# A spectral mixer and token MLP on one core: first transform copied out of PSUM two tiles at a time, in a hand-written order, with fixed PSUM banks and smaller units in the middle

## Chip, cores, metric

The kernel runs on one core of a Trainium2 chip. The metric is the device time of one execution in microseconds (us), median of several runs; lower is better. The profile's span is some 1.5 to 1.8 us shorter than the device time and starts with the first instruction. PSUM is the memory, in eight banks, into which PE writes its results. Engines: PE multiplies matrices, DVE (VectorE), ACT (ScalarE) and POOL (GpSimd) work elementwise, SP issues most loads.

## The reference

```python
x = A_x                                           # [1, 2048, 512], bf16
h = x + A(layernorm(x), w_r, w_i)                 # A: rfft2 over (2048, 512), times W = w_r + i w_i, irfft2
h2 = h + B(layernorm(h), w1, b1, w2, b2)          # B: gelu(h^T w1 + b1) w2 + b2 over the 2048 tokens, F = 1376
```

## The kernel before

The Fourier transforms are products with constant matrices. The stages that matter here, with the program's names:

- **Front.** Sixteen tiles X (128 x 512) are loaded. The mean goes away by itself in the transform; the norm factor rs is made per tile (DVE or ACT), and the constant FP is scaled by it into FS (POOL, ACT or DVE). f1 = four matmuls per tile into PSUM (ps); Y = copy of ps to SBUF.
- **Middle**, eight units of four groups: f2 (matmuls on Y, result copied to CS), x (matmuls on CS), V = ps times W (DVE, reading PSUM), g1 (matmuls on V, result copied to PQ by ACT).
- **Residual stage**, sixteen tiles: g2, EO copy, g3, then on DVE two residual adds (TT), H, and HH = normalised H; ACT makes squares (JK) and the factor r.
- **Two large products** on PE with GELU between (w1, w2), until the end.

A small list scheduler in the kernel orders all instructions: it takes, again and again, the operation that can start first by its estimates of durations, and picks a PSUM bank for it. Only this order is compiled; each engine works off its own list strictly in that order. Besides the real matmuls, PE's list of the front holds 32 on a tile of zeros, called fillers or zero matmuls here: they keep PE busy so that its granted clock stays full (what happens without them is seen in e3 below).

```python
N_WARM = 20                                         # matmuls on a tile of zeros before the first real one
WARM_AFTER = (4, 3, 2, 1, 1, 0, 1, 0, ...)          # and behind tile 0, 1, 2 ... of the first transform
...
for q in range(8):                                  # front: per pair of tiles and half b, one copy of 512
    for b in range(2):
        unit = PsumUnit("f1", 1)
        for n in range(2):
            mm(f"f1_{n2}_{b}a", ...); mm(f"f1_{n2}_{b}b", ...)
        if (q, b) in Y_DVE: dve(f"y_{q}_{b}", ... tensor_copy ..., 512, prio=28)
        else:               act(f"y_{q}_{b}", dst, src, ACT.Copy, 512, prio=28)
        ... warm(f"warmf{q}{n}{w_}", wu, 13, after=[lastmm[n]])
...
def stage_x(u):                                     # middle: eight matmuls, then V in one or two operations
    unit = PsumUnit("x", 2)
    grp = [cs_ops[2 * u + 1]]
    ...
    nh = 2 if u in V_SPLIT else 1                   # V_SPLIT = (0, 7)
...
def act(...):
    return K.op(name, "act", emit, ..., occ=lat - 90.0, lat=lat + 50.0, ...)   # the scheduler's estimate for ACT
```

Of the kernel before, what the change touches and what calls it, by code (L numbers as in the profile page):

```python
# [6 lines left out]
ACT = mybir.ActivationFunctionType  # L7
ALU = mybir.AluOpType
LN_EPS = 1e-5
NP = 128  # L10
S_LEN = 2048
D_LEN = 512
# [24 lines left out]
def _row(sign, comp, k2, s):  # L37
    return 4 * (k2 * 2 + s) + 2 * sign + comp
# [52 lines left out]
def build_consts():  # L91
# [22 lines left out]
    fp = fp.reshape(NP, NS2, NP)  # L114
    fp = np.stack([-fp, fp], axis=2)
# [26 lines left out]
    c["E"] = e.reshape(NP, 1024)  # L142
    c["MR"] = np.concatenate([m.reshape(NP, 512), r.reshape(NP, 512)], axis=1)
# [5 lines left out]
PSUM_BANKS = 8  # L149
CELL = 4  # L150
# [28 lines left out]
class Builder:  # L179
    def __init__(self, nc, limits):  # L180
        self.nc = nc
        self.ops = []
        self.writer = {}
        self.readers = {}
        self.tensors = {}
        self.limits = limits
        self.cell_cache = {}

# [37 lines left out]
    def op(self, name, engine, emit, ins=(), outs=(), occ=100.0, lat=None, unit=None, pr=False, pw=False,  # L226
           first=False, last=False, prio=0, nbytes=0, is_dma=False, not_before=0.0, after=(), group=None, rate=DMA_RATE):
# [13 lines left out]
        o.rate = rate  # L241
        deps = {id(d): d for d in after}
# [38 lines left out]
    def schedule(self):  # L281
# [13 lines left out]
        order = []  # L295
        while len(order) < len(ops):
            best = None
            for o in ready:
                bank, avail = None, 0.0
                u = o.unit  # L300
                if u is not None and not u.claimed:
# [5 lines left out]
                    for b in range(PSUM_BANKS - u.nbanks + 1):  # L307
                        if all(bank_unit[i] is None for i in range(b, b + u.nbanks)):
                            t = max(bank_free[b:b + u.nbanks])
                            if cand is None or t < cand[0]:  # L310
                                cand = (t, b)
# [10 lines left out]
            ready.remove(o)  # L322
            o.sched, o.start = True, st
# [11 lines left out]
            if o.is_dma:  # L335
                x0 = max(st + (3200.0 if st < 4000.0 else 1700.0), dma_free)
                dma_free = x0 + o.bytes / o.rate
                o.finish = dma_free + 200.0
            else:
                o.finish = st + o.lat  # L340
# [86 lines left out]
def memory_layout():  # L427
# [26 lines left out]
    add("W", [NP, NG, 2, LW], bf, rw)  # L454
    add("HH", [NP, NS2, D_LEN], bf, rw)
# [29 lines left out]
RS_GROUPS = ((0,), (2,), (4,), (5,), (6, 7), (8, 9), (10, 11), (12,), (13,), (14,), (15,))  # L485
FS_ENG = {4: "act", 7: "act", 9: "dve", 11: "dve", 13: "dve", 14: "act", 15: "dve"}
Y_DVE = ((5, 1), (6, 1), (7, 1))
N_WARM = 20
WARM_AFTER = (4, 3, 2, 1, 1, 0, 1, 0, 0, 0, 0, 0, 0, 0, 0, 0)
V_SPLIT = (0, 7)  # L490
# [4 lines left out]
def build_kernel(nc, A_x, A_w_r, A_w_i, B_w1, B_b1, B_w2, B_b2, out):  # L495
# [5 lines left out]
    K = Builder(nc, {"f1": 6, "f2": 2, "x": 2, "g1": 2, "g2": 2, "g3": 2, "mm1": 5, "mm1b": 6, "mm2": 8})  # L501
# [3 lines left out]
    X, FS, Y, CS, V, PQ, EO, H, HH, GT, OUT, W = (T[n] for n in ("X", "FS", "Y", "CS", "V", "PQ", "EO", "H", "HH", "GT", "OUT", "W"))  # L505
# [9 lines left out]
    def dma(name, dst, src, nbytes, stream="sp", outs=(), ins=(), prio=0, strided=False, after=(), group=None, rate=DMA_RATE,  # L515
            not_before=0.0):
        def emit(eng, bank):
            if strided:
                with nc.allow_non_contiguous_dma(reason="small bias gather"):
# [3 lines left out]
                    rate=rate, occ=1000.0 if stream == "pool" else 640.0 if rate < DMA_RATE else 460.0, not_before=not_before)  # L523
# [10 lines left out]
    def act(name, dst, src, func, n, ins=(), outs=None, unit=None, prio=0, last=True, psum=True, bias=None, scale=None, accum=None):  # L534
# [15 lines left out]
        return K.op(name, "act", emit, ins=ii, outs=oo, occ=lat - 90.0, lat=lat + 50.0, unit=unit, pr=unit is not None,  # L550
# [13 lines left out]
    def ldf(q, pr_, stream="sp", nb=0.0):  # L564
        sl = slice(4 * q, 4 * q + 4)
        dma(f"ld_FP{q}", FP[:, sl, :, :], cin[f"FP{q}"][:, :, :, :], 1 << 18, outs=[FP[:, sl, :, :]], prio=pr_, stream=stream, not_before=nb)

    for q, (a, b) in enumerate(((0, 2), (2, 4), (4, 6), (6, 8), (8, 12))):
        ldx(a, b, 90 - q)
    ldf(2, 84)  # L570
    ldx(12, 16, 83)
    ldf(3, 82)
    ldf(0, 90, "act")
    act("table", T["tb"][:, 0:1], EPS[:, 0:1], ACT.Abs_reciprocal_sqrt, 1, ins=[EPS[:, 0:1]], prio=88)
    ldf(1, 87, "act", 1800.0)
    dma("ld_E", EM[:, 0:1024], cin["E"][:, :], 1 << 18, outs=[EM[:, 0:1024]], prio=44)
    dma("ld_MR", EM[:, 1024:2048], cin["MR"][:, :], 1 << 18, outs=[EM[:, 1024:2048]], prio=43)
    wload = {}
    for ch, (u0, u1) in enumerate(((0, 1), (1, 4), (4, 8))):
        g0, ng = 4 * u0, 4 * (u1 - u0)  # L580
        lst = []
        for w, dram in ((0, A_w_r), (1, A_w_i)):
            for comp in range(2):
                d = W[comp::4, g0:g0 + ng, w, :]
                lst.append(dma(f"ld_wp{ch}_{w}{comp}", d, bass.AP(dram.tensor, g0 * LW, [[64 * LW, 32], [LW, ng], [1, LW]]),
                               32 * ng * 514, prio=42 - ch, group=f"w{ch}", rate=300.0))
                h0, nh = (g0, ng) if g0 else (1, ng - 1)
                d = W[2 + comp::4, h0:h0 + nh, w, :]
                lst.append(dma(f"ld_wm{ch}_{w}{comp}", d, bass.AP(dram.tensor, (64 - h0) * LW, [[64 * LW, 32], [-LW, nh], [1, LW]]),
                               32 * nh * 514, prio=42 - ch, group=f"w{ch}", rate=300.0))  # L590
                if g0 == 0:
                    d = W[2 + comp::4, 0, w, :]
                    lst.append(dma(f"ld_wz{ch}_{w}{comp}", d, bass.AP(dram.tensor, 32 * LW, [[64 * LW, 32], [1, LW]]),
                                   32 * 514, prio=42 - ch, group=f"w{ch}", rate=300.0))
        for u in range(u0, u1):
            wload[u] = lst
    dma("ld_D2", EM[:, 2048:3072], cin["D2"][:, :], 1 << 18, outs=[EM[:, 2048:3072]], prio=30)
    dma("ld_IF", IF[:], cin["IF"][:, :, :], 1 << 19, outs=[IF[:]], prio=29)
    w1src = B_w1.rearrange("(p s2) f -> p s2 f", s2=NS2)
    for q in range(4):  # L600
        sl = slice(4 * q, 4 * q + 4)
        dma(f"ld_w1_{q}", W1[:, sl, :], w1src[:, sl, :], 4 * F_LEN * 2 * NP, outs=[W1[:, sl, :]], prio=28 - q, after=wload[7][-1:])
# [13 lines left out]
    ZT, BV = T["ZT"], T["bv"]  # L616
    K.op("zt", "dve", lambda eng, bank: eng.memset(ZT[:, :], 0.0), outs=[ZT[:, :]], occ=200.0, prio=60)  # L617
# [9 lines left out]
    def fs_op(i):  # L627
        e = FS_ENG.get(i, "pool")
        rs = RS[:, i:i + 1]
        if e == "act":  # L630
            act(f"fs{i}", FS[:, i, :, :], FP[:, i, :, :], ACT.Copy, 256, ins=[FP[:, i, :, :]], scale=rs, prio=30)
        else:
            dve(f"fs{i}", lambda eng, bank: eng.tensor_scalar(FS[:, i, :, :], FP[:, i, :, :], rs, None, op0=ALU.mult),  # L633
                [FP[:, i, :, :], rs], [FS[:, i, :, :]], 120, prio=30, engine=e, lat=920.0 if e == "pool" else None)

    def stat_act(i):
# [3 lines left out]
        nm = NM[:, i:i + 1]  # L640
        dve(f"nm_{i}", lambda eng, bank: eng.tensor_scalar(nm, SM[:, i:i + 1], -1.0 / D_LEN, None, op0=ALU.mult), [SM[:, i:i + 1]], [nm], 1, prio=33, engine="pool", lat=210.0)
        dve(f"bv_{i}", lambda eng, bank: eng.tensor_scalar(BV[:, i:i + 1], nm, nm, LN_EPS, op0=ALU.mult, op1=ALU.subtract), [nm], [BV[:, i:i + 1]], 1, prio=33, engine="pool", lat=210.0)
        act(f"rs_{i}", RS[:, i:i + 1], V1[:, i:i + 1], ACT.Abs_reciprocal_sqrt, 1, ins=[V1[:, i:i + 1]], bias=BV[:, i:i + 1],
            scale=-1.0 / D_LEN, prio=32)
        fs_op(i)

    def stat_dve(grp):
        a, b = grp[0], grp[-1] + 1
        for i in grp:
# [3 lines left out]
            dve(f"st_{i}", lambda eng, bank, i=i, x=x: eng.bn_stats(ST[:, i, 0:6], x), [x], [ST[:, i, 0:6]], 512, prio=25)  # L653
# [15 lines left out]
    Yv = Y[:].rearrange("p b y g (n k) -> p b (y g) n k", k=4)  # L669
    for q in range(8):  # L670
        for b in range(2):
            unit = PsumUnit("f1", 1)
            lastmm = {}
            for n in range(2):
                n2 = 2 * q + n
                lo = X[:, n2, b * NP:b * NP + NP]
                hi = X[:, n2, 256 + b * NP:256 + b * NP + NP]
                f = FS[:, n2, 1, :]
                f2 = bass.AP(f.tensor, f.offset, [list(f.ap[0]), [0, 2], [1, NP]])
                fm = FS[:, n2, :, :]  # L680

                def o(bank, n=n):
                    return ps[:, bank, n * 256:n * 256 + 256]
                mm(f"f1_{n2}_{b}a", o, lo, f2, unit, True, False, n == 0, 14, 256, ins=[lo, f])
                lastmm[n] = mm(f"f1_{n2}_{b}b", o, hi, fm, unit, False, True, False, 14, 256)

            def src(bank):
                v = ps[:, bank, :].rearrange("p (n g k) -> p n g k", n=2, k=4)
                return v.rearrange("p n g k -> p g n k")
            dst = Yv[:, b, :, 2 * q:2 * q + 2, :]  # L690
            if (q, b) in Y_DVE:
                dve(f"y_{q}_{b}", lambda eng, bank, dst=dst, src=src: eng.tensor_copy(dst, src(bank)), [], [dst], 512, unit=unit, prio=28)
            else:
                act(f"y_{q}_{b}", dst, src, ACT.Copy, 512, unit=unit, prio=28)
            for n in range(2):
                for w_ in range(WARM_AFTER[2 * q + n] if b == 1 else 0):
                    warm(f"warmf{q}{n}{w_}", wu, 13, after=[lastmm[n]], last=2 * q + n == LAST_WARM)
# [3 lines left out]
    def stage_f2(u):  # L701
        for i in range(2):
            G = 2 * u + i
            unit = PsumUnit("f2", 1)
            for par in range(2):
                for b in range(2):
                    mm(f"f2_{G}_{par}{b}", lambda bank, par=par: ps[:, bank, par * 256:par * 256 + 256],
                       Y[:, b, par, 2 * G:2 * G + 2, :].rearrange("p g k -> p (g k)"), E[:, b, par, :],
                       unit, b == 0, b == 1, par == 0 and b == 0, 10, 256)
            dst = CS[:, G, :, :, :].rearrange("p y c j -> p (y c j)")  # L710
            if G == 1:
                cs_ops[G] = dve(f"cs_{G}", lambda eng, bank, dst=dst: eng.tensor_copy(dst, ps[:, bank, :]), [], [dst], 512, unit=unit, prio=14)
            else:
# [167 lines left out]
```

## Time and profile before

| | us |
|---|---|
| device time, median (lowest to highest) of the 4 runs beside the changed kernel | 134.07 (133.96 to 134.32) |
| traced span | 132.36 |
| first V starts | 21.49 |
| V stage (first V to end of last V) | 17.88 |
| from there to the first residual add | 3.27 |
| first residual add to last HH (its start) | 26.25 |
| last HH to the end | 63.47 |

The five rows below the span add up to it; they come from the list of single instructions. (The table in the prediction was cut where the chain changes engine, so its last two stretches differ from these.) The chain of waits and the table by stretch stand in the prediction. The granted clock is 1.00 in all stretches of the prediction's table.

### The profile page before, as it was taken

How to read it: one execution, taken by the hardware profiler on the slowest of the kernel's cores; microseconds unless marked ns; L12 is line 12 of the kernel's file. 1: busy time of each engine (PE TensorE's matmuls, PEld its weight loads, DVE VectorE, ACT ScalarE, POOL GpSimd, SP SyncE). 2: the span in 40 equal slices, each digit the busy share in tenths (PEclk: the TensorE clock that was granted, in tenths of full speed). 3: DMA queues.
4: the chain of work that ended last, by engine and by line, in shares of the span. 5: the costliest groups of instructions: out<-in, count | busy, mean ns of one | idle time of the engine just before them, and what ended most of it. 6: DMA issues, size and time to landing. Idle time of an engine off the chain costs nothing.

```text
span 132.4 us, 2013 instructions
## 1 busy us (share of the span) xinstructions
PE 123.7 (93%) x776; PEld 74.5 (56%) x786; DVE 69.3 (52%) x127; ACT 63.3 (48%) x146; POOL 12.4 (9%) x33
## 2 busy tenths in 40 slices
PE   6989989999977979999999999999999999999990
PEld 2436656788666736544434444456666666666660
DVE  0499867999981999999960000000242332423322
ACT  4579976978966999986689322222000000000000
POOL 0199920000300000000000000000000000000000
PEclk9999999999999999999999999999999999999999
DMA  2999699999999999992000000000111112111121
GB/s 80 375 396 364 153 244 273 286 322 283 419 426 417 410 408 411 417 295 74 0 0 0 0 0 0 5 0 0 40 40 70 49 40 82 42 57 62 40 79 40
DMA packets 16648, 22.16 MB, mean 167 GB/s; under 512 B 2720, under 2 KB 12960, under 8 KB 16128
## 3 DMA queue, kind: packets, MB, share of 16 engines
q1 hardware_dynamic: 16352, 21.52, 47.5%
q10 hardware_dynamic: 288, 0.52, 1.1%
q8 instruction: 6, 0.10, 0.3%
q14 instruction: 2, 0.02, 0.0%
HBM read 19.95 MB, written 2.10 MB: 167 GB/s over the span
## 4 chain that ended last, share of the span: by engine, by line
PE 51%; DVE 32%; ACT 9%; DMA 3%; POOL 2%; issue 1%; DVEq 0%; ACTq 0%
PE ps L531 50%; DVE V L739 13%; DVE H L799 7%; ACT Y L549 5%; DVE TT L790 4%; DVE TT L792 4%; DVE HH L804 4%; DMA X<-in_A_x_dram 3%; POOL FS L633 1%; ACT rs L549 1%; ACT FS L549 1%; ACT JK L549 1%; DVE OUT L829 1%; ACT PQ L549 0%; PE ps L621 0%
## 5 line engine op out<-in xcount | busy, mean ns | idle before, releaser
L531 PE MATMUL ps<-HH,W 128*128 128x512 bf16 (+1 forms) x173 | 40.3, 379 | 1.3 <-DVE HH L804 0.9
L531 PE MATMUL ps<-GT,W 128*128 128x512 bf16 (+1 forms) x172 | 37.9, 379 | 0.2
L829 DVE SCALAR_TENSOR_TENSOR OUT<-ps,B2f,H 128x512 bf16<-128x512 f32 x16 | 12.0, 750 | 48.7 <-PE ps L531 48.7
L531 PEld LDWEIGHTS ps<-GT,W 128*128 128x128 bf16 (+1 forms) x176 | 25.3, 144 | 12.8
L531 PEld LDWEIGHTS ps<-HH,W 128*128 128x128 bf16 (+1 forms) x176 | 17.2, 100 | 21.2 <-DVE HH L804 1.9
L739 DVE TENSOR_TENSOR V<-ps,W 128x2048 bf16<-128x2048 f32 (+1 forms) x10 | 17.9, 1856 | 0.9 <-PE ps L531 0.9
L549 ACT ACTIVATE GT<-ps,B1f 128x512 bf16<-128x512 f32 (+1 forms) x11 | 7.1, 689 | 14.6 <-PE ps L531 14.6
L549 ACT ACTIVATE JK<-H,nm 128x512 bf16<-128x512 bf16 x16 | 11.6, 722 | 3.0 <-DVE H L799 2.9
L653 DVE BATCH_NORM_STATS2 st<-X 128x6 f32<-128x512 bf16 x14 | 9.2, 669 | 4.1 <-DMA X<-in_A_x_dram 4.1
L621 PE MATMUL ps<-ZT 128*128 128x512 bf16 x32 | 9.6, 434 | 1.6 <-DVE ZT L617 1.2
L799 DVE TENSOR_TENSOR H<-ps,TT 128x512 bf16<-128x512 f32 x16 | 10.9, 682 | 0.0
L549 ACT ACTIVATE PQ<-ps 128x512 bf16<-128x512 f32 x16 | 8.9, 602 | 3.5 <-PE ps L531 3.3
L531 PE MATMUL ps<-EM,PQ 128*128 128x256 bf16 x64 | 9.0, 273 | 0.8 <-ACT PQ L549 0.7
L531 PE MATMUL ps<-EM,V 128*128 128x128 bf16 x128 | 9.2, 219 | 0.5 <-DVE V L739 0.5
L549 ACT ACTIVATE EO<-ps 128x512 bf16<-128x512 f32 x16 | 9.2, 596 | 0.9 <-PE ps L531 0.9
L549 ACT ACTIVATE CS<-ps 128x512 bf16<-128x512 f32 x15 | 8.3, 607 | 2.1 <-PE ps L531 2.1
L531 PE MATMUL ps<-EM,Y 128*128 128x256 bf16 x64 | 8.7, 273 | 0.4 <-ACT Y L549 0.4
L531 PE MATMUL ps<-FS,X 128*128 128x256 bf16 x64 | 8.4, 274 | 0.5 <-POOL FS L633 0.4
L531 PEld LDWEIGHTS ps<-EM,V 128*128 128x128 bf16 x128 | 7.5, 98 | 2.3 <-issue 1.4
L633 POOL TENSOR_SCALAR FS<-FP,rs 128x256 bf16<-128x256 bf16 x9 | 8.6, 965 | 0.6 <-ACT rs L549 0.5
L790 DVE TENSOR_TENSOR TT<-ps,X 128x256 f32<-128x256 f32 x16 | 6.7, 417 | 3.3 <-PE ps L531 3.3
L531 PEld LDWEIGHTS ps<-EM,PQ 128*128 128x128 bf16 x64 | 6.2, 98 | 2.9 <-ACT PQ L549 0.9
(36 smaller groups left out, 79.1 us busy)
## 6 DMA issues: line engine op xcount, KB each, us to landing
W<-in_B_w_dram SPq DMA_DIRECT2D x4, 1376.0 KB, 11.7
W<-in_B_w_dram SPq DMA_DIRECT2D x10, 512.0 KB, 18.3
out_dram<-OUT SPq DMA_DIRECT2D x16, 128.0 KB, 1.7
W<-in_A_w_r_dram SPq DMA_DIRECT2D x4, 257.0 KB, 4.5
W<-in_A_w_i_dram SPq DMA_DIRECT2D x4, 257.0 KB, 5.0
X<-in_A_x_dram SPq DMA_DIRECT2D x4, 256.0 KB, 5.0
X<-in_A_x_dram SPq DMA_DIRECT2D x2, 512.0 KB, 6.6
W<-in_A_w_r_dram SPq DMA_DIRECT2D x4, 192.8 KB, 3.3
```

What stands on the lines that cost most here:

```text
L531: return K.op(name, "pe", lambda eng, bank: eng.matmul(outf(bank), lhsT, rhs, start=start, stop=stop), ins=ins or [lhsT, rhs], occ=occ, la ...
L549: return eng.activation(dst, s, func, **kw)
L621: return K.op(name, "pe", lambda eng, bank: eng.matmul(ps[:, bank, :], ZT[:, 0:NP], ZT[:, :], start=True, stop=True), ins=[ZT[:, :]], occ= ...
L633: dve(f"fs{i}", lambda eng, bank: eng.tensor_scalar(FS[:, i, :, :], FP[:, i, :, :], rs, None, op0=ALU.mult), [FP[:, i, :, :], rs], [FS[:, ...
L653: dve(f"st_{i}", lambda eng, bank, i=i, x=x: eng.bn_stats(ST[:, i, 0:6], x), [x], [ST[:, i, 0:6]], 512, prio=25)
L739: return eng.tensor_tensor(vout, s, win, ALU.mult)
L790: dve(f"tl_{s2}", lambda eng, bank, tt=tt, xl=xl: eng.tensor_tensor(tt[:, 0, :], ps[:, bank, 256:512], xl, ALU.add), [xl], [tt[:, 0, :]], ...
L792: dve(f"th_{s2}", lambda eng, bank, tt=tt, xh=xh: eng.tensor_tensor(tt[:, 1, :], xh, ps[:, bank, 256:512], ALU.subtract), [xh], [tt[:, 1, ...
L799: return eng.tensor_tensor(hs.rearrange("p (h d) -> p h d", h=2), e, tt[:, :, :], ALU.add)
L804: dve(f"hh_{s2}", lambda eng, bank, s2=s2, hs=hs: eng.tensor_scalar(HH[:, s2, :], hs, NM[:, s2:s2 + 1], R2[:, s2:s2 + 1], op0=ALU.add, op1 ...
L829: dve(f"fin{s2}", lambda eng, bank, dst=dst, bia=bia, hs=hs: eng.scalar_tensor_tensor(dst, ps[:, bank, :], bia, hs, op0=ALU.add, op1=ALU.add),
```

## The change

The intent: copies out of PSUM of two tiles at once (fewer, larger ACT operations), an order of the front written by hand, a shorter way from the last Y copy to the first V (half copies, four x matmuls, V of 512), half copies for the last unit, fewer load issues, and PSUM banks fixed by class so that stages don't block each other. The cut below leaves out that the scheduler's estimates of loads changed as well, and that the norm of the two tiles done on ACT needs one POOL step less.

```diff
+CLASS_BANKS = {"x": (4, 6), "f2": (0, 1, 2, 3), "g1": (0, 1, 2, 3)}
...
-RS_GROUPS = (..., (6, 7), (8, 9), (10, 11), (12,), (13,), (14,), (15,))
-FS_ENG = {4: "act", 7: "act", 9: "dve", 11: "dve", 13: "dve", 14: "act", 15: "dve"}
-Y_DVE = ((5, 1), (6, 1), (7, 1))
+RS_GROUPS = (..., (6, 7), (8,), (9, 10), (11, 12), (13,), (14, 15))
+FS_ENG = {3: "act", 4: "act", 9: "dve", 11: "dve", 13: "dve", 14: "dve", 15: "dve"}
+Y_EVAC = (("pair", "act"), ("pair", "act"), ("pair", "act"), _AA, ("pair", "act"), ("single", ("act",), ("dve",)), _AA, ("single", ("act",), ("dve", "act")))
+FRONT = {"dve": "bn_0 ag_0 bn_2 ...", "act": "s1_1 s2_1 rs_0 ... yp_0 rs_6 yp_1 rs_8 yp_2 ...", "pool": "...",
+         "pe": "f1_0 f1_1 f1_3 f1_4 f1_2 f1_5 ..."}
 N_WARM = 20
 WARM_AFTER = (4, 3, 2, 1, 1, 0, 1, 0, 0, 0, 0, 0, 0, 0, 0, 0)
-V_SPLIT = (0, 7)
+V_SPLIT = (7,)
...
+    K.forced = {e: FRONT[e].split() for e in ("dve", "act", "pool")}      # the scheduler must keep this order
+    K.forced["pe"] = [f"{n}_{b}{h}" for n in FRONT["pe"].split() for b in range(2) for h in "ab"]
...
-        return K.op(name, "act", emit, ..., occ=lat - 90.0, ...)
+        return K.op(name, "act", emit, ..., occ=lat - 120.0, ...)
...
+    dma("ld_EMR", ...)                              # one load instead of two
+    # first W chunk: own tile W0, 8 issues instead of 12; w1 in eight parts, D2 and IF in two
...
+            split = u == 0                          # stage_f2: CS of unit 0 in halves, ACT and DVE
+            if i == 0 or u == 0:                    # stage_x: unit 0 in two groups of four x matmuls,
+                    K.op(f"v_0_{i}{w}", "dve", ...) #          V of unit 0 from W0 in four operations of 512
+            split = (u, h) == (7, 1)                # stage_g1: last PQ copy in halves, DVE and ACT
...
+    for j, n2 in enumerate(f1_order):
+        for w_ in range(WARM_AFTER[j]):
+            warm(f"warmf{j}{w_}", wu, 13, after=[lastmm[n2]])
```

## The prediction

> **What bounds the kernel now.** I read the chain that ended last first, then the table of busy time by stretch, cut where the chain changes engine, and then the groups with shapes kept apart. The chain, in order of time (start us, us, what):
>
> ```profile
> 8.76 0.31 POOL bv L642
> ...
> 17.10 1.47 ACT Y L549 x3
> 18.57 0.05 issue
> 18.62 2.77 PE ps L531 x25
> ...
> 21.48 1.04 DVE V L739
> ...
> 22.62 15.62 DVE V L739 x8
> ...
> 40.13 0.61 ACT PQ L549
> 40.74 0.05 issue
> 40.78 1.82 PE ps L531 x14
> ```
>
> From 9.15 us on ACT holds the chain until its last Y copy at 18.57; then PE (with a CS copy inside) until 21.48; then the ten V multiplies on DVE. The table by stretch (us, then each engine's busy us):
>
> ```profile
> 9.35:18.62 9.27, 8.70 (x65) 5.61 (x65) 8.28 (x26) 9.18 (x25) 7.67 (x14) 1.00 0.90 271
> 18.62:21.48 2.86, 2.86 (x27) 2.00 (x28) 1.00 (x2) 1.69 (x3) 0.00 (x0) 1.00 0.92 241
> 21.48:39.37 17.89, 16.92 (x224) 13.01 (x223) 17.88 (x10) 14.04 (x27) 1.22 (x7) 1.00 1.08 339
> 39.37:42.63 3.26, 2.57 (x25) 2.05 (x25) 0.00 (x0) 2.04 (x5) 0.00 (x0) 1.00 1.02 427
> 42.63:68.05 25.42, 24.10 (x133) 12.73 (x134) 25.33 (x63) 22.01 (x60) 0.00 (x0) 1.00 0.71 267
> 68.05:132.40 64.35, 60.87 (x277) 35.90 (x282) 12.42 (x17) 9.17 (x15) 0.00 (x0) 1.00 0.10 33
> ```
>
> So the bound moves: ACT (9.18 of 9.27), a hand-over of 2.86, DVE (17.88 of 17.89), a hand-over of 3.26, DVE (25.33 of 25.42), PE. The change touches the first four stretches, 39.4 us. The other 90 us (residual adds and norm on DVE, the two large products on PE) keep instructions and sizes; they can only start earlier. The forms that matter:
>
> ```profile
> L739 DVE TENSOR_TENSOR V<-ps,W 128x2048 bf16<-128x2048 f32 x6 | 13.3, 2281 | 0.0
> L549 ACT ACTIVATE Y<-ps 128x512 bf16<-128x512 f32 x13 | 7.0, 607 | 0.0
> L739 DVE TENSOR_TENSOR V<-ps,W 128x1024 bf16<-128x1024 f32 x4 | 4.7, 1218 | 0.9 <-PE ps L531 0.9
> L692 DVE CAST Y<-ps 128x512 bf16<-128x512 f32 x3 | 2.1, 692 | 0.7 <-PE ps L531 0.6
> ```
>
> These durations overlap their neighbours. What counts in a full queue is the step from start to start in the list of single instructions: Y on ACT 0.478 us, V of 2048 elements 2.197, V of 1024 1.13, a one-column ACT op 0.185, FS on ACT 0.40, FS on POOL 0.925 (1.0 beside a DVE FS).
>
> **What the Trainium skill says.** (1) "Perfetto Trace Analysis", Optimizing Scalar/DVE Operations, gives an access overhead per instruction of about 51 ns for Scalar and 125 ns for DVE on PSUM, and says that larger operations help a saturated engine. ACT agrees: 0.478 - 512/1.2 GHz (0.427) = 0.051. DVE shows half: 2.197 - 2048/0.96 GHz (2.133) = 0.064; I use 0.064. (2) The same section says that where Scalar or Vector is not saturated but makes bubbles on others, smaller instructions let work finish sooner. The stretches 18.62 to 21.48 and 39.37 to 42.63 are that case: ACT is busy 1.69 of 2.86 and 2.04 of 3.26 us. (3) "VectorE: DVE Perf Modes", Why PSUM operands drop a tier, holds fp32 PSUM inputs to one element per cycle; the 2.197 us agree, so a new layout of V cannot make a V op faster per element. (4) "TensorE: Matmul & The Clock Gate", Why this matters for your kernels, warns of PE gaps over about 3 us; the granted clock is 1.00 in every stretch here.
>
> **The change, part by part.**
>
> *Y copies.* Before: 13 on ACT and 3 on DVE of 512. After, from the order of instructions: on ACT four of 1024, six of 512 and one of 256; on DVE one of 512 and one of 256. ACT gets 4x1024 + 6x512 + 256 = 7424 elements instead of 6656: 768 x 0.833 ns = 0.64 us more, less two fixed parts (0.10). One FS leaves ACT (-0.40) and one small rs op too (-0.19). Net about zero. So pairing in itself does not shorten ACT's queue; what could is ACT starting on Y earlier.
>
> It does start earlier. POOL's bv now follows directly on sm, so one POOL step is gone, and the second norm of the ACT pair finishes at about 8.24 us instead of 9.45. Walking the new order with the steps above (semaphores at what the trace shows: 0.034 us ACT to DVE, 0.09 ACT to POOL, 0.055 to PE, 0.04 from PE): FS 3 and 4 on ACT at 8.27 and 8.98, pairs at 9.57, 10.66 and 11.75, singles of tiles 6 and 7 at 12.84 and 13.31. Then ACT waits. POOL's FS of tile 8 ends at 13.4 (POOL runs without a gap from 7.8), its matmuls at 14.35, and the pair of tiles 8 and 9 starts at 14.39 instead of 13.98. Single 10 at 15.54; 12, after POOL's FS at 15.33, at 16.03; the joined rs of 14 and 15 at 16.51. FS 14 and 15 on DVE at 16.85 and 17.05, their matmuls until 17.8 and 18.2, single 14 at 17.83, and the two halves of tile 15 end at 18.47 (DVE) and 18.70 (ACT). Before, the last two copies ended at 18.57 and 18.94 (DVE). **The front ends only about 0.24 us earlier**: the early start is spent on waits, and fewer, larger pieces make each wait longer.
>
> *First middle unit.* Before: last Y copy 18.94, V at 21.485: 2.55 us, for 15 matmuls, a 512 DVE copy and eight x matmuls. After: the first half-group's matmuls end 0.33 and 0.44 us after the last copy; a 256 copy on DVE lasts 0.69 - 256/0.96 GHz = 0.42; PE reaches the first four x matmuls at +1.0 (eight f2 at 0.109, then the 0.2 us that the trace shows between f2 and x), and V comes 0.53 later (0.75 for eight x before, less two steps of 0.11). Sum 1.58, **a gain of 0.96**. First V at 18.70 + 1.58 = 20.28.
>
> *V stage.* Four V of 512 (0.597 each) replace two of 1024 (1.13): +0.13. V of unit 1 needs 13 more f2 and eight x after the second small unit; on PE's order it is ready at about 22.85, and DVE is free at 22.67: +0.2. Then six steps and two halves as before. The last V ends at about 38.5 (before 39.365): **0.2 to 0.4 lost** of the gain.
>
> *Last unit.* The last g1 result is evacuated in halves on DVE and ACT: the half on ACT takes 0.597 - 256/1.2 GHz = 0.38 instead of 0.60: **-0.21**.
>
> *Loads.* The first W chunk goes out in 8 issues of about 0.64 us instead of 12, and E, M and R as one: SP is about 3 us earlier with what follows. No V waits for W now, and W1 is needed no earlier than its gain. Off the path.
>
> Sum: -0.24 - 0.96 + 0.13 + 0.2 - 0.21 = -1.08; with some 0.1 for PE waits in the V stage, -1.0 us. The 90 us after it move as a block: **134.13 - 1.0 = 133.1 us**.
>
> **The rivals.** *PE becomes the bound of the middle.* At the first V, PE has done 12 of 64 f2 and 4 of 64 x; before it was 21 and 8. So 9 x 0.109 + 0.25 = 1.2 us of PE work moves into a stretch that DVE filled by itself. Up to its last x, PE has 64 f2 (7.0), 8 x groups (0.55 each, 4.4) and 96 g1 (0.056 each, 5.4): 16.8 us from f2's start, against about 18.4 us from there to the last unit's V. It fits, but x of unit 5 comes close: I count 12.0 us of PE work ahead of it, and it is wanted at about 12.3. Waits of 0.2 to 0.6 could add up: 133.3 to 133.7. For it speaks that V of unit 6 already waited for x (step 2.262, not 2.197); against it, that f2's order was chosen anew for this.
>
> *The front goes better or worse than my walk.* Runs of four bf16 elements in the single copies are new, and so are the strides across banks in the pairs. If ACT or DVE slowed for that by a fifth, six singles cost 0.6 us: 133.7. If the waits at tiles 8 and 14 close up, the front gains another 0.6: 132.5. POOL, the slowest per tile, makes that unlikely, since tile 12 still needs its ninth FS.
>
> *The gain is hidden.* If a W chunk or W1 were late, the earlier start would meet a DMA wait: 134. The waits show no DMA ahead of V or of the large product, and the loads go out earlier as well.
>
> **Range and chances.** Front +-0.3, hand-over +-0.2, V stage +0.5 or -0.2, and the three runs before spread by 0.36: 132.3 to 133.9 holds it 8 times in 10. Faster by over 2% means below 131.4, which needs 1.7 us more than any part offers: 0.05. Slower by 2% (136.8) needs a stage that breaks, such as a clock drop: 0.02.
>
> **What would show it.** Right: last Y copy at 18.5 to 18.9 with ACT waiting for PE before the pair of tiles 8 and 9; a first V of 512 elements near 20.3; DVE without gaps over 0.3 us until 38.5; first residual add near 41.6; stretches after it as long as before. Wrong: Y steps over 0.5 per 512 elements, an x or g1 wait of DVE in mid-stage adding to more than 0.6, a V that waits for W0, a granted clock below 1, or a DVE stage after 41.6 unlike 25.4 us.

## The result, and the profile after

The changed kernel is correct. Four runs of it took 135.34 to 136.35 us, median 136.11; the four runs of the kernel before on the same chip 133.96 to 134.32, median 134.07. The ratio is 1.014, 95% interval 1.0095 to 1.0184. A ratio here is the mean time of one kernel's fast runs over that of the other's fast runs of the same rounds, so it is not quite the ratio of the medians. The kernel is slower, and 136.11 lies outside my range of 132.3 to 133.9.

| us | before | after | difference | predicted |
|---|---|---|---|---|
| end of last Y copy | 18.94 | 20.21 | +1.27 | -0.24 |
| from there to first V | 2.55 | 1.74 | -0.81 | -0.96 |
| V stage | 17.88 | 18.60 | +0.72 | +0.43 |
| to the first residual add | 3.27 | 3.13 | -0.14 | -0.21 |
| first residual add to last HH | 26.25 | 26.89 | +0.64 | 0 |
| last HH to the end | 63.47 | 63.61 | +0.14 | 0 |
| traced span | 132.36 | 134.18 | +1.82 | -1.0 |

The same cuts in the table of busy time by stretch of the changed kernel (us; then each engine's busy us with the number of instructions for PE, PE's weight loads, DVE, ACT, POOL; then granted clock, DMA share, GB/s):

```profile
9.93:20.21 10.28, 8.99 (x66) 5.89 (x66) 7.21 (x24) 8.46 (x17) 6.87 (x14) 1.00 1.15 325
20.21:21.95 1.74, 1.74 (x16) 0.92 (x15) 0.86 (x3) 0.71 (x2) 0.00 (x0) 1.00 1.21 291
21.95:40.54 18.59, 18.06 (x236) 14.08 (x234) 18.21 (x12) 14.97 (x29) 1.28 (x7) 1.00 1.05 346
40.54:43.67 3.13, 2.65 (x26) 2.07 (x25) 0.43 (x2) 1.84 (x5) 0.00 (x0) 1.00 1.02 418
43.67:70.56 26.89, 25.58 (x140) 12.79 (x139) 25.68 (x63) 22.99 (x63) 0.00 (x0) 1.00 0.58 207
70.56:134.18 63.62, 60.30 (x279) 35.58 (x277) 12.44 (x17) 8.39 (x12) 0.00 (x0) 1.00 0.10 33
```

ACT, which filled the front before (9.18 of 9.27), now is busy 8.46 of 10.28: it waits. In the V stage PE is as full (18.06 of 18.59) as DVE. The residual stage has the same instructions and 0.64 us more.

One caution on the first row. The first zero matmuls take 0.427 us each, and from some moment on 0.216; call this the full clock. It came at 4.13 us in the trace before and at 6.25 in the one after. In a1 below, which has the same front as the changed kernel, it came at 3.99, and the last Y copy ended at 19.73 instead of 20.21: so some 0.5 us hangs on that moment. Two later runs with the old front and the new loads ended it at 18.62 (d1, full clock at 4.09) and 19.02 (e1, 6.24). At like clocks the new front is thus 1.1 to 1.2 us later than the old one, so the 1.27 isn't luck.

The chain of waits of the changed kernel, in order of time (start us, us, what), tells what ACT waits for. Line 648 is the helper of the zero matmuls, line 553 that of all real ones:

```profile
1.17 6.97 PE ps L648 x20
8.14 0.45 PE ps L553 x4
8.63 0.82 PE ps L648 x3
9.45 0.44 PE ps L553 x4
9.89 0.88 PE ps L648 x4
10.77 1.32 PE ps L553 x12
12.12 1.02 ACT Y L571
...
20.12 13.51 PE ps L553 x163
33.66 4.50 DVE V L824 x2
```

The chain begins with PE, not with ACT: 20 zero matmuls, 4 real ones, 3 zero, 4 real, 4 zero, 12 real, and only then ACT's second pair copy at 12.12. My walk had that copy at 10.66. From 20.12 to 33.66 the chain stays on PE, where the kernel before had DVE's V. The kernel before has fillers between the first tiles too (PE's list, line 621 the zero ones):

```profile
7.52 0.61 PE L531 MATMUL ps<-FS,X 128*128 128x256 bf16 x4 [0.42 <-POOL FS L633]
8.19 0.82 PE L621 MATMUL ps<-ZT 128*128 128x512 bf16 x3
8.85 0.60 PE L531 MATMUL ps<-FS,X 128*128 128x256 bf16 x4
9.28 0.83 PE L621 MATMUL ps<-ZT 128*128 128x512 bf16 x3
10.03 0.61 PE L531 MATMUL ps<-FS,X 128*128 128x256 bf16 x4
```

There they cost little: leaving them out brought the first V only 0.3 us forward (b3 and d3 below).

### The profile page after: what moved, and what is told of

Same layout as the page of the kernel before. It is cut to its first block, busy times and chain, and to the rows that moved or that the text cites. A ratio compares the mean times of both kernels' runs of the same rounds, so it can differ in the third digit from the quotient of the medians.

```text
span 134.2 us, 2029 instructions
## 1 busy us (share of the span) xinstructions
PE 126.0 (94%) x786; PEld 74.9 (56%) x786; DVE 69.8 (52%) x131; ACT 63.6 (47%) x143; POOL 12.1 (9%) x32
## 4 chain that ended last, share of the span: by engine, by line
PE 69%; DVE 14%; ACT 12%; issue 3%
PE ps L553 62%; PE ps L648 7%; ACT JK L571 4%; DVE H L899 4%; DVE V L824 3%; ACT Y L571 3%; ACT EO L571 3%; DVE HH L904 2%; DVE TT L890 2%; DVE TT L892 2%; ACT r L571 1%; ACT PQ L571 1%; DVE OUT L929 1%; ACT rs L571 1%; DVE FS L660 0%
## 5 line engine op out<-in xcount | busy, mean ns | idle before, releaser
L553 PE MATMUL ps<-HH,W 128*128 128x512 bf16 (+1 forms) x176 | 41.0, 379 | 1.3 <-DVE HH L904 1.1
L824 DVE TENSOR_TENSOR V<-ps,W 128x2048 bf16<-128x2048 f32 (+1 forms) x8 | 15.7, 2019 | 0.4 <-PE ps L553 0.2
L648 PE MATMUL ps<-ZT 128*128 128x512 bf16 x34 | 11.0, 467 | 1.4 <-DVE ZT L591 1.2
L571 ACT ACTIVATE PQ<-ps 128x512 bf16<-128x512 f32 (+1 forms) x16 | 9.1, 590 | 3.7 <-PE ps L553 3.6
L571 ACT ACTIVATE CS<-ps 128x512 bf16<-128x512 f32 (+1 forms) x16 | 8.4, 575 | 1.5 <-PE ps L553 1.5
L571 ACT ACTIVATE Y<-ps 128x512 bf16<-128x512 f32 (+2 forms) x11 | 7.7, 731 | 2.2 <-PE ps L553 2.2
L553 PEld LDWEIGHTS ps<-FS,X 128*128 128x128 bf16 x64 | 5.9, 98 | 3.7 <-DVE FS L660 2.0
```

What stands on the lines that cost most here:

```text
L553: return K.op(name, "pe", lambda eng, bank: eng.matmul(outf(bank), lhsT, rhs, start=start, stop=stop), ins=ins or [lhsT, rhs], occ=occ, la ...
L571: return eng.activation(dst, s, func, **kw)
L648: return K.op(name, "pe", lambda eng, bank: eng.matmul(ps[:, bank, :], ZT[:, 0:NP], ZT[:, :], start=True, stop=True), ins=[ZT[:, :]], occ= ...
L824: return eng.tensor_tensor(vout, s, win, ALU.mult)
```

## The experiments

My theory after the two traces had three parts. (1) The zero matmuls stand in PE's list ahead of real ones, so the hand-written order of the front comes late. (2) The small first unit moves PE work behind the first V and makes DVE wait in the V stage. (3) The scheduler, with another estimate for ACT, wrote another order in the residual stage. The rivals: the new copies are slower (excluded at once by the trace: the pair of 1024 takes 1.02 us, and pairs follow each other after 1.09 as in my walk; the singles step by 0.478 as before), the fixed banks cause the waits, or the loads do. All times are medians, with the lowest and highest run in brackets; the ratio is to the kernel before in the same rounds. Except for c2, which is wrong, every kernel was correct.

| run | time | ratio [95%] |
|---|---|---|
| changed kernel | 136.11 (135.34 to 136.35) | 1.0140 [1.0095, 1.0184] |
| a1_stage_order | 135.44 (134.53 to 135.65) | 1.0100 [1.0063, 1.0137] |
| a2_warm14 | 135.27 (135.17 to 135.30) | 1.0095 [1.0069, 1.0122] |
| a3_nowarm | 134.44 (134.36 to 134.61) | 1.0036 [1.0009, 1.0062] |
| a4_middle_only | 133.87 (133.76 to 134.37) | 1.0000 [0.9970, 1.0029] |
| b1_both_undone | 133.78 (133.72 to 133.81), fast runs | 0.9968 [0.9949, 0.9986] |
| b2_x_earlier | 134.36 (134.26 to 134.59) | 1.0015 [0.9996, 1.0033] |
| b3_before_nowarm | 134.82 (134.80 to 134.87) | 1.0046 [1.0028, 1.0064] |
| b4_old_front_nowarm | 133.71 (133.66 to 133.77), fast runs | 0.9964 [0.9946, 0.9982] |
| c1_free_banks | 134.57 (133.93 to 134.88) | 1.0013 [0.9988, 1.0039] |
| c2_half_g1 (wrong) | 133.58 (133.24 to 135.17) | 0.9985 [0.9938, 1.0033] |
| c3_whole_first | 135.22 (134.89 to 135.57) | 1.0083 [1.0062, 1.0103] |
| c4_whole_nowarm | 134.83 (134.69 to 135.66) | 1.0055 [1.0030, 1.0079] |
| d1_whole_banks | 134.68 (134.54 to 134.82) | 1.0049 [1.0030, 1.0068] |
| d2_whole_nowarm_banks | 134.59 (134.55 to 134.96) | 1.0042 [1.0021, 1.0062] |
| d3_before_nowarm_banks | 134.18 (133.62 to 135.08) | 1.0018 [0.9987, 1.0050] |
| e1_whole_banks2 | 133.86 (133.75 to 134.25) | 0.9974 [0.9949, 0.9998] |
| e2_whole_nowarm2 | 133.93 (133.74 to 134.26) | 0.9979 [0.9957, 1.0002] |
| e3_small_nowarm | 133.86 (133.66 to 134.23) | 0.9973 [0.9950, 0.9997] |

b1 and b4 each had one run slow (137.03 and 136.78 us, mean granted clock 0.946 and 0.951). It was the profiled one in both, so no trace of these two is used. Their cause is open; no other kernel here had such a run, so the figures of b1 and b4 hold for their fast runs alone.

### The residual stage: a1_stage_order

```diff
+STAGE = {"act": "eo_0 ... r2_2 q_3 eo_9 r2_3 q_4 eo_10 ...", "dve": "... tl_3 h_2 hh_0 th_3 ...", "pe": "g2_0_10 ..."}
+    for e in STAGE: K.forced[e] = K.forced[e] + STAGE[e].split()      # the order of the kernel before
```

> The changed kernel with one thing undone: in the stage of the residual adds and the second norm, ACT, DVE and PE get the order of instructions that they had in the kernel before (the scheduler had made another). Everything ahead of it is as in the changed kernel. Theory (the new order makes DVE wait for ACT's norm factors, and costs 0.63 us from the first residual add to the last norm multiply: 26.89 against 26.25 us): that stage is 26.2 to 26.3 us again, and the kernel 0.6 us faster than the changed one, about 135.5 us. Rival (the stage is longer because of loads that share memory with it, or because it starts at another time): the stage stays at 26.9 us, 136.1 us.

In the list of instructions the changed kernel has HH of tile 0 ahead of H of tile 2 on DVE (before: behind it), and on ACT the EO copies from tile 9 on ahead of the squares. In the groups of HH, before and after (count, busy us, mean ns, idle ahead of it), first the kernel before, then the changed one:

```profile
L804 DVE TENSOR_SCALAR HH<-H,nm,r 128x512 bf16<-128x512 bf16 x16 | 6.5, 406 | 0.9 <-ACT r L549 0.9
```

```profile
L904 DVE TENSOR_SCALAR HH<-H,nm,r 128x512 bf16<-128x512 bf16 x16 | 6.5, 409 | 1.2 <-ACT r L571 0.9
```

DVE idles 0.3 us more ahead of HH, in five new waits (HH of tiles 0, 3, 4, 6 and 7, 0.02 to 0.13 us each), and each wait also costs the overlap of about 0.085 us that two DVE operations without a wait have (an H of 0.68 us is followed after 0.60 us). That makes 0.7, less some 0.1 for shorter delays that only the kernel before has: about the 0.64. With the old order written down, the stretch of a1 is:

```profile
43.20:69.45 26.25, 24.92 (x137) 13.12 (x139) 25.33 (x64) 22.79 (x63) 0.00 (x0) 1.00 0.63 228
```

26.25 us, as in the kernel before; in a2 and a3 below, which keep the new order, it stayed at 26.88. So the order is the cause of the 0.64. The time is 0.67 us below that of the changed kernel, measured in another batch in which the kernel before took 134.03 instead of 134.07; the two intervals overlap, so it is the trace and not the time that shows this. That the scheduler chose the order because of its new estimate (lat - 120 for lat - 90) is what the diff suggests; I did not test it by itself, and its estimates of loads changed too.

### The front: a2_warm14 and a3_nowarm

```diff
-N_WARM = 20                                           # a2: changed kernel with
+N_WARM = 14
```

```diff
-WARM_AFTER = (4, 3, 2, 1, 1, 0, 1, 0, ...)            # a3: changed kernel with
+WARM_AFTER = (0,) * 16
```

> The changed kernel with 14 instead of 20 matmuls on zeros at PE's start, nothing else. Theory (PE is late at the first transform because its queue runs the 20 at half clock until 6.2 us, and everything behind it moves with it): the first real matmul comes at 7.2 us instead of 7.98, the second pair copy on ACT at about 11.3 instead of 12.12, the first V multiply at about 21.1 instead of 21.95, the kernel 0.6 to 0.8 us faster, 135.4 us. If in its run the clock rises early (4.1 us), little is gained in that trace. Rival (the norm factors on ACT and the scaled matrices on POOL set the pace, PE only follows): the first V stays at 21.8 to 22.0 us.

> The changed kernel without the 12 matmuls on zeros between the matmuls of the first transform; the 20 at the start stay. Theory (they lie in PE's queue ahead of the matmuls that the pair copies wait for, 4 of them ahead of tile 3 alone, 0.87 us): the second pair copy at 11.0 instead of 12.12 us, first V at 20.7 to 21.0 us, the kernel 1.0 us faster, 135.1 us. Rival 1 (they only fill time in which PE would wait for the scaled matrices): first V as now, 21.95. Rival 2 (without them the granted clock falls to half in the first transform): matmul steps of 0.21 instead of 0.11 us and a slower kernel.

In a2 the first real matmul ran at 7.13 us instead of 7.97, the first V at 21.11 instead of 21.95, and the time became steady (spread 0.13 us instead of 1.0). But the full clock came early in this trace (3.97 us); against a1, where it came as early, the first V (21.47) gains 0.36 us. The rest of the 0.84 is the clock's moment. That the steady times come from runs in which the full clock is late is likely, but no trace of a2 shows such a run. In a3, PE's list from 5.9 to 11 us is short (start us, us, engine, line, operation, count):

```profile
5.41 2.72 PE L648 MATMUL ps<-ZT 128*128 128x512 bf16 x10
7.97 3.17 PE L553 MATMUL ps<-FS,X 128*128 128x256 bf16 x24
```

The first real matmul is as late as in the changed kernel (7.97), but then 24 run in 3.17 us with no zero matmuls between. The second pair copy starts at 10.46 (my walk: 10.66), the first V at 20.39 (my walk: 20.28). The full clock came as late as in the changed kernel (6.24 us), so the two traces can be compared. So the twelve zero matmuls between the real ones account for 1.56 of the 1.67 us by which the walk missed the first V, and the walk's durations were right: its last Y copy was to end at 18.70 and ended at 18.64. The V stage (18.60) and the residual stage (26.88) stayed as in the changed kernel.

### What the parts are worth: a4_middle_only, b1_both_undone, b4_old_front_nowarm

```diff
 # a4: the front of the kernel before (its copies, order and zero matmuls), loads and middle of the changed kernel,
 #     residual stage in the order of the kernel before
 # b1: a1, and N_WARM = 14, WARM_AFTER = (0,) * 16
 # b4: a4, and N_WARM = 14, WARM_AFTER = (0,) * 16
```

> The first transform as in the kernel before (its copies, its order on all four engines), the loads, the middle stage with the small first and last units and the fixed banks as in the changed kernel, the later stage in the order of before. Theory (the middle part of the change is worth about what was predicted less the PE waits that the trace of the changed kernel shows, and the loss is in the front and in the later stage's order): first V at 20.4 to 20.6 us, V stage 18.3 to 18.6 us, later stage 26.25 us, the kernel at 133.2 to 133.7 us, faster than before by 0.4 to 0.9 us. Rival (the middle part itself loses what it gains, through PE): 134.1 us or more.

> The changed kernel with both suspected costs taken away: no zero matmuls between the first transform's matmuls and 14 instead of 20 at the start; in the later stage the order of the kernel before. If these two are the whole miss, they add: first V at 20.3 to 20.4 us, later stage 26.25 us, end of the traced span at 131.9 us, the kernel at 133.7 us, faster than before by 0.3 to 0.4 us. Rival (a third cost, or the two overlap): 134.2 us or more.

> As b1_both_undone, but with the first transform of the kernel before (512 copies, its order). Tells what the pair copies and the hand-made order are worth when PE is not in their way. Theory (ACT's sum is the same in both and the waits eat the early start, as the prediction had it: 0.24 us for the new front): first V 0.1 to 0.4 us later than in b1_both_undone, 20.5 to 20.7 us, kernel 0.1 to 0.4 us slower than b1. Rival (the new front is worth nothing): same first V and same time.

a4 is as fast as the kernel before. In its trace the way from the last Y copy to the first V is 1.67 us instead of 2.55, so the small first unit does gain 0.87, close to my 0.96; and its V stage is 18.60 us instead of 17.88, which takes nearly all of it back. b1 undoes both losses of the changed kernel and is faster than the kernel before by 0.3%. b4 has the old copies and the old order of the front, and is as fast as b1 (133.71 and 133.78 in the same rounds). So the pair copies and the hand-written order are worth nothing measurable here; my 0.24 for them is not confirmed.

### The waits in the V stage: b2_x_earlier, c1_free_banks, c2_half_g1

```diff
 # b2: b1, PE's list of the middle written down with x of units 1, 5 and 7 some matmuls earlier
 # c1: a4, orders of the middle written down, and
-CLASS_BANKS = {"x": (4, 6), "f2": (0, 1, 2, 3), "g1": (0, 1, 2, 3)}
+CLASS_BANKS = {}
 # c2: a4, orders written down, one g1 matmul of each two left out
-                    for w in range(2):
+                    for w in range(1):
```

> As b1_both_undone, and in PE's order of the middle stage the x matmuls of units 1, 5 and 7 are moved ahead of matmuls that no V multiply waits for, and the third f2 pair ahead of the second small x. Theory (the three waits of DVE in the V stage, 0.32, 0.19 and 0.13 us, come from PE's order alone): V stage 18.0 to 18.1 us instead of 18.60, kernel 0.5 us faster than b1_both_undone, about 133.2 us. Rival (PE has too much work for the stretch, whatever its order): V stage stays at 18.4 us or more, the waits only move.

> a4_middle_only with the order of every engine in the middle written down as it was there, and the PSUM banks free instead of fixed (first transform's results on six banks, x on four pairs, g1 on six). If the waits of the V stage (0.32, 0.19 and 0.13 us before units 1, 5 and 7 in the changed kernel) came from the fixed banks, the V stage falls from 18.60 to about 18.0 us and the time to about 133.3. If they come from the work on PE, which was busy 17.85 of 18.60 us there, banks change nothing: V stage 18.5 to 18.7, time 133.9. I expect the second.

> a4_middle_only with the second of each two g1 matmuls left out, the rest in its order (wrong result on purpose): 48 of 96 matmuls of 128 columns go, some 2.7 us of PE work out of 17.85. If the amount of PE work makes the waits of the V stage, it is 18.0 to 18.1 us (ten steps of DVE and two more operations, no waits over 0.05) and the time about 133.3. If the waits are those of single hand-overs (a result that is late whatever PE has to do besides), the V stage stays above 18.4. I expect the first.

In the changed kernel V of units 1, 5 and 7 start 0.32, 0.19 and 0.13 us later than a full DVE queue would let them. In b2 the wait at unit 1 is gone, and V of units 3, 5, 6 and 7 start 0.24, 0.40, 0.28 and 0.24 us late: V stage 19.12. The waits moved and grew; the theory that this order would remove them fell, and I tried no other. In c1, with free banks, the V stage is 19.06, with waits at units 1, 3, 5 and 7 (0.33, 0.15, 0.48 and 0.13 us): freeing the banks doesn't help while the order is the one written for the fixed banks. An order of its own for free banks stays untested (c3 below shows that order and banks hang together). In the changed kernel's own trace x of units 1, 5 and 7 started 0.7, 1.6 and 1.6 us after the V that frees their pair of banks had ended, so these x did not wait for their own banks. The profiled run of c1 also got its full clock only at 7.38 us, so its time says less than its V stage.

The lists of DVE's V operations, first of the changed kernel, then of c2 (start us, us, ..., idle time ahead of the group and what ended it):

```profile
21.94 2.48 DVE L809 TENSOR_TENSOR V<-ps,W 128x512 bf16<-128x512 f32 x4 [0.32 <-PE ps L553]
24.66 15.88 DVE L824 TENSOR_TENSOR V<-ps,W 128x2048 bf16<-128x2048 f32 x8 [0.23 <-PE ps L553]
```

```profile
20.55 2.48 DVE L811 TENSOR_TENSOR V<-ps,W 128x512 bf16<-128x512 f32 x4 [0.32 <-PE ps L589]
23.26 15.54 DVE L826 TENSOR_TENSOR V<-ps,W 128x2048 bf16<-128x2048 f32 x8 [0.23 <-PE ps L589]
```

With half of the g1 matmuls gone, the eight later V take 15.54 us instead of 15.88 (a4, from which c2 is made, has 15.88 too): the waits at units 5 and 7 are gone. The wait ahead of unit 1 stays at 0.23 (0.32 with the lost overlap), since no g1 runs before it. So the later waits come from the amount of PE work, as I expected, and the first one does not, which I had not expected: it comes from the f2 and x matmuls that the small first unit leaves for after the first V (in c3 and d1 below, with that unit whole again, it is gone). V stage 18.26, where I expected 18.0 to 18.1. The time isn't conclusive: two of the six runs had a clock of 0.987 and took 135.1 us.

### The first unit whole again: c3_whole_first, c4_whole_nowarm, d1_whole_banks, d2_whole_nowarm_banks, e1_whole_banks2, e2_whole_nowarm2, e3_small_nowarm

```diff
 # c3: a4 with the first unit as before; V of unit 0 stays four operations of 512 from W0; PE's middle in the old order
-            split = u == 0
+            split = False
-            if i == 0 or u == 0:
+            if i == 0:
 # c4: c3, and N_WARM = 14, WARM_AFTER = (0,) * 16
 # d1, d2: c3, c4 with every PSUM bank as the kernel before had it
+BANKS = {"f1_0_0a": ..., "f2_0_00": 2, "x_0_00": 6, ...}
 # e1, e2: d1, d2 without a fixed bank for the second half of the last g1 result
-    ... g1_30_00:6 g1_31_00:6
+    ... g1_30_00:6
 # e3: b4 again, in the rounds of e1 and e2
```

> a4_middle_only with the first unit of the middle whole again (copies of 512, one group of eight x matmuls), PE in the order of the kernel before; W0, fixed banks and the split last unit stay, and V of unit 0 stays four operations of 512. If the small first unit only shifts PE work behind the first V, this gets 0.9 us later to the first V (about 21.3 to 21.5) and has a V stage of 18.0 to 18.1: time within 0.3 us of a4 (133.87), so 133.8 to 134.2. If the V stage's waits have another source, it stays at 18.6 and the time is 134.6 to 134.8.

> c3_whole_first with 14 zero matmuls at the start and none between the first transform's matmuls, so b4_old_front_nowarm with a whole first unit. Of the change only the loads, W0, the fixed banks and the last unit are left. If the loads are what lets an earlier first V be used (b3, with the old loads, waited 0.45 us for W), then first V at 21.1 to 21.3, V stage 18.0 to 18.1 without a wait for W, time 133.7 to 134.0, as good as b4 (133.73) within 0.3. If the small first unit is worth something by itself, it is over 134.1.

c3 and c4 missed: 135.22 and 134.83. The V stage was 18.82 in both. The wait at unit 1 was gone, but V of unit 6 waited 0.69 us for PE. PE's list had been written for other banks: x of unit 4 could use a third pair of banks in the kernel before and ran 5.97 us after the first V; with two fixed pairs it had to wait for V of unit 2 and ran at 7.03. It was not a clean undoing, so I repeated it with the old banks.

> c3_whole_first with every PSUM bank of the first two stages written down as in the kernel before. If the bank was what spoilt c3, x of unit 4 runs about 6.0 us after the first V, the V stage is 18.0 to 18.1 us (17.88 and 0.13 for two more operations) and the time 133.9 to 134.2. Then the small first unit's net worth is this time less that of a4 (133.87). If the new loads or the order of something else did it, the V stage stays at 18.8 and the time at 135.2.

> c4_whole_nowarm with the same banks. First V at 21.1 to 21.2, V stage 18.0 to 18.1 without a wait for a load, time 133.6 to 133.9, as good as b4 (133.73). If the small first unit is worth 0.3 us or more by itself, it is over 134.0.

In d1 x of unit 4 is back at 5.97 us, and DVE's V operations have no wait but the first:

```profile
21.17 2.48 DVE L827 TENSOR_TENSOR V<-ps,W 128x512 bf16<-128x512 f32 x4 [0.93 <-PE ps L601]
23.57 15.53 DVE L842 TENSOR_TENSOR V<-ps,W 128x2048 bf16<-128x2048 f32 x8
```

V stage 17.93 in d1 and d2. But the hand-over after the last V was 3.75 us instead of 3.13, because of a fault of mine, which one line of d1's list shows (PE, the second half of the last g1 result):

```profile
40.13 0.40 PE L601 MATMUL ps<-EM,V 128*128 128x128 bf16 x4 [0.52 <-DVE PQ L873]
```

My list of banks put both halves into one bank, and the second waited for the copy of the first.

> d1_whole_banks with a bank of its own for the second half of the last g1 result. V stage 17.93 as in d1, hand-over back from 3.75 to 3.13 us, time 134.05 (134.68 less 0.62). Small first unit with 20 and 12 zero matmuls worth about 0.2 us (a4: 133.87).

> d2_whole_nowarm_banks with the same bank freed. First V 21.15, V stage 17.93, hand-over 3.13, time 133.95. If the small first unit gains 0.87 us and gives back the waits of 0.6 us, e3 is 0.2 to 0.3 us faster than this; if it is worth the 0.96 less 0.4 of my prediction, e3 is 0.5 to 0.6 us faster.

> b4_old_front_nowarm once more: 133.73 in fast runs; first V at 20.2, V stage 18.6, hand-over 3.13, later stage 26.25 at a clock of 1.00. Some runs may fall to a clock of 0.95 and be some 3 us longer, as one of b4 and one of b1 did.

With that bank free, e1 takes 133.86 and e2 133.93 us (V stage 17.93, hand-over 3.06), and e3, the small first unit in the same rounds, 133.86. The ratios to the kernel before are 0.9979 for e2 and 0.9973 for e3. So the small first unit is worth 0.07 us or nothing: it gains about 0.87 us ahead of the first V, loses 0.67 (18.60 less 17.93) behind it and 0.07 at the next hand-over (3.13 less 3.06). I had expected 0.2 to 0.3 of it to remain; the traces leave 0.13, and the times do not show even that.

Part of the reason may be the clock, as e3's own trace shows. Its table by stretch in the front (columns as above, clock third from the end):

```profile
8.00:11.00 3.00, 1.48 (x11) 0.86 (x12) 3.00 (x11) 2.33 (x8) 2.91 (x5) 0.99 1.04 406
11.00:14.00 3.00, 3.00 (x17) 2.13 (x15) 2.70 (x9) 2.73 (x7) 2.47 (x3) 0.50 1.06 362
14.00:17.00 3.00, 3.00 (x28) 2.53 (x26) 2.35 (x8) 3.00 (x11) 2.63 (x6) 0.94 1.20 295
```

The granted clock fell to half for some 3.4 us from about 10.95 us on, after PE had been busy 1.48 of 3 us, and the first V came at 20.81; that run took 134.23 us, the others of e3 133.66 to 133.95. d2's profiled run did the same. In both the mean clock of the run is 0.987, and this mark can be counted. With the zero matmuls between the real ones none of 94 runs (49 of the kernel before, 45 of the changed one, a1, a2, a4, c1, c3, d1 and e1) has a mean clock below 0.99. Without them 6 of 57 fast runs have 0.983 or 0.987: one each of c4, d2, e2 and e3, with 14 at the start, and two of d3, with 20. (Two runs of c2 have it as well, with the zero matmuls but half of the g1 work; where they lost it isn't known.) So the zero matmuls between the real ones are not for nothing: without them some runs lose the clock. a3 and b3, with 20 at the start, showed no such run in twelve.

### The loads: b3_before_nowarm and d3_before_nowarm_banks

```diff
 # b3: the kernel before, order of all else written down, with
-WARM_AFTER = (4, 3, 2, 1, 1, 0, 1, 0, ...)
+WARM_AFTER = (0,) * 16
 # d3: b3 with every PSUM bank as the kernel before had it
```

> The kernel before without its 12 zero matmuls between the first transform's matmuls; the order of everything else kept. Theory (in the kernel before they lie in time in which PE waits anyway, since ACT's queue of copies sets the end of the front): first V at 21.4 to 21.5 us, kernel as before, 134.0 us within 0.2. Rival (the zero matmuls cost in any order): first V more than 0.5 us earlier, 133.4 us or less.

> b3_before_nowarm with the same banks: the kernel before, only without the twelve zero matmuls between the first transform's. If the old loads do not carry an earlier V stage, V of unit 4 waits 0.3 to 0.5 us for its W chunk, the V stage is 18.2 to 18.4 and the time 134.1 to 134.3, so nothing is won by the zero matmuls alone. If the loads are off the path, as I predicted, the V stage is 17.9 and the time 133.8.

Both bring the first V to 21.2 us, 0.3 earlier than the kernel before, and neither wins anything: b3 is slower (134.82, but there the banks had changed too), d3 is the same within its interval. In d3's list of DVE's V operations:

```profile
21.20 8.95 DVE L802 TENSOR_TENSOR V<-ps,W 128x1024 bf16<-128x1024 f32 x5 [0.94 <-PE ps L594]
31.57 8.95 DVE L802 TENSOR_TENSOR V<-ps,W 128x2048 bf16<-128x2048 f32 x5 [1.43 <-DMA W<-in_A_w_i_dram]
```

V of unit 4 waits 1.43 us for the last chunk of W. SP's issues of these loads (shortest/median/longest ns, first and last start us), of the kernel before, of the changed kernel, and of d3:

```profile
L521 SPq DMA_DIRECT2D W<-in_A_w_i_dram x14: 598/623/1041, 9.8 to 24.7; - x14
```

```profile
L543 SPq DMA_DIRECT2D W<-in_A_w_i_dram x12: 599/623/835, 7.7 to 21.3; - x12
```

```profile
L584 SPq DMA_DIRECT2D W<-in_A_w_i_dram x14: 599/623/2327, 9.7 to 26.4; - x14
```

In the kernel before the last issue starts at 24.7 us, the load lands at 30.11, and V of unit 4 starts at 30.35, with no wait: 0.24 us were left. In d3 one issue took 2.33 us, the last started at 26.4 and landed at 31.55, and V was late by 1.4. With four issues fewer the changed kernel starts the last one at 21.3 (landed at 28.01). No trace of a kernel with the new loads shows a wait of V for W. That is why the new loads matter: they are what allows an earlier V stage to be used; what they save by themselves was not tested. How late the old loads are differs from run to run (V of unit 4 waited 0.45 us in b3's trace, 1.43 in d3's); why that one issue took 2.33 us stays open.

## Why the prediction was wrong, step by step

**The front, predicted 0.24 us earlier, measured 1.27 later.** This is the step that failed most. "The front ends only about 0.24 us earlier" came from a walk in which PE took a real matmul as soon as its FS was there. The walk left out 32 zero matmuls that stand in PE's list. The hand-written list names only real matmuls; the zero ones fall in by the scheduler's estimates, and in the new order three and then four of them (0.82 and 0.88 us in the chain) came ahead of tiles that ACT's pair copies wait for. There were fillers in the old order too; as I read the two chains, the earlier start on ACT made PE's list the one that is waited for. a3 removes the twelve between, and the walk then holds within 0.11 us. The 20 at the start add to it in runs in which the full clock comes late: at half clock each takes 0.427 us.

**First middle unit, predicted -0.96, measured -0.81 in the changed kernel and -0.87 in a4.** Right in its mechanism. The terms as written do not quite add up: eight f2 at 0.109 and the 0.2 behind them are 1.07, not 1.0, and with 0.53 make 1.60 where the sum says 1.58; measured were 1.74 and 1.67.

**V stage, predicted +0.43, measured +0.72.** The mechanism was named, as a rival as well: PE work moves behind the first V. The term was too small. I gave 0.2 to the wait at unit 1 (measured 0.32) and 0.1 to all later waits together (0.19 at unit 5 and 0.13 at unit 7). Together they pass the 0.6 that I had named as a sign of being wrong. c2 shows that the later ones come with PE's load. I counted 12.0 us of PE work ahead of x of unit 5 against 12.3 us of time; it is about this narrow, and it came late. The two more V operations cost 0.05 us net in d1 (17.93 against 17.88, where the kernel before had a wait of 0.07 at unit 6).

**Last unit, predicted -0.21, measured -0.14**, and in e1 and e2 3.06, so -0.21.

**Loads, "off the path".** True in that no V waited for W before or after; but wrong as a judgement of what the part is for. The last chunk had only 0.24 us to spare, and d3 shows that the old loads would have met an earlier V stage with waits up to 1.4 us.

**"The 90 us after it move as a block."** They did not. I knew that a scheduler writes the order and that its estimate for ACT had changed in the diff, and compared instructions and sizes but not the order of that stage. It cost 0.64 us (a1). The last 0.14 us, from the last HH to the end, stand in every fast trace with the new loads (63.6 against 63.47); I did not test what makes them.

The sum: my -1.0 missed the measured +1.82 by 2.8 us, of which the front is 1.51, the residual stage and the end 0.78, the V stage 0.29, the hand-overs 0.22. Undoing the two largest (b1) gives 133.78 us in fast runs, 0.3% better than the kernel before; e1 (old front, new loads, whole first unit, old banks) and b4 are as good, and all three beat both kernels in fast runs. What these three have in common are the new loads, V of unit 0 in four operations and the halved copy of the last unit. The halved copy shows as 3.06 to 3.13 for 3.27 us. The loads may help the front too: in d1 the first real matmul ran at 7.21 us, in the kernel before at 7.52, with the full clock at 4.09 and 4.13. I did not test these apart, so how the 0.3% splits stays open.

## What to carry to other kernels

Walk every engine's own list to the end, with the filler instructions in it: a hand-written order of real work is worth nothing if fillers placed by a rule stand between. Where a scheduler orders the program, compare the order of all stages, not only of those that the diff names; an estimate changed for one stage moves another. Work that a smaller first piece leaves for later lands on the engine that feeds the next stage, so count that engine's load up to each hand-over before counting the gain.

## What the Trainium skill lacked or had wrong

- "TensorE: Matmul & The Clock Gate" (What's actually happening; Why this matters for your kernels) puts the change to full clock after about 3.4 us of sustained work, varying by 500 ns, and warns of gaps over about 3 us. In the twelve traces of kernels with 20 zero matmuls at the start (the first at 1.17 us), the full clock came at 3.99 to 7.38 us, a range of 3.4 us; and in e3 the clock fell to 0.50 although PE's longest gap was 1.5 us, after six microseconds in which PE was busy 2.9. The page's free-running window agrees with the range; its 500 ns do not, and its gap rule is not enough by itself (the page also tells of short idle times, if frequent, that cost the clock).
- "Perfetto Trace Analysis" (Optimizing Scalar/DVE Operations): 125 ns for DVE on PSUM; the V steps here, with one input in PSUM, show about 64 (2.197 us for 2048 elements, 1.13 for 1024). Its advice of smaller pieces held for the hand-over (-0.87 us), but the page lacks that the engine that feeds the next stage can pay it back (+0.67 us in the V stage).
- No page that I read says what filler matmuls cost in PE's list: here twelve of them delayed the first V by 1.56 us.
- No page that I read says how load issues on SP slow down: most took 0.62 us, single ones 1.04 to 2.33, and behind the longest of them V waited 1.43 us.
